# Two schedule lists of a fused attention and gated-MLP kernel: first scores at step 7, last splits from step 9

## The chip, the core and the metric

The kernel runs on one core of a Trainium2 chip. The metric is the device time of one execution in microseconds (us). The core's engines run their own instruction queues in order and wait for each other through semaphores: TensorE (PE, matrix products; PEld is its weight load), VectorE (DVE), ScalarE (ACT), GpSimd (POOL) and SyncE (SP), which here issues every DMA.

## What is computed

Three stages, one after the other. Packed attention: per batch (8) and head (8), 32 learned queries p attend to 576 keys, and then 576 queries q attend to the 32 results. A gated MLP with an RMS norm follows, and then a bilinear layer with two matrices behind it.

```python
p_packed = sm_attn(p, k, v)              # 32 rows per head
out = sm_attn(q, p_packed, p_packed)     # 576 rows per head
x = out as (4608, 512)
xn = x / rms(x) * rms_g
x = (silu(xn @ w_gate) * (xn @ w_val)) @ w_out
a = x @ w1
b = x @ w2
result = (a * b @ w3) @ w_out2
```

The large weights arrive as 64-bit numbers and are converted on the chip. Products that need more than one pass of the fast format are made from a high and a low part ("split": ACT rounds to the high part, DVE or POOL subtracts it to get the low one).

## The kernel before

The first stage is a loop over the 8 batches (`dense_units(b)`, line 362). A batch has 48 units, two to a tile of 128 rows and 288 columns of the hidden layer: an even unit is the gate, an odd unit the value. Each unit is six matmuls of 128x288 into one PSUM bank of a pool of four (tag `gv`, line 376). An even unit is then read by ACT (tanh, line 382, `th`) and by DVE (line 383); an odd unit is read by ACT (`vl`, line 387) and multiplied on POOL (`ht`, line 388). Groups of 8 units share one pair of weight tiles `wbh`/`wbl`; after the fourth unit of a group `wb_unit` (line 330) makes the next group's with 16 small matmuls (line 337) into a slot of the second PSUM pool (tag `at`, two slots of two banks), and splits it in two halves: ACT `wbh` (L55), DVE `wbl` (L56).

Other work is put between the units by hand. `planned(main, (steps, generator), ...)` (line 431) lets the main generator emit unit n, and then, for each list in which n stands, lets that list's generator emit its next piece. So a list entry n means: behind unit n and ahead of unit n+1 in the queue of every engine that the piece uses. In batch b these are:

- `pack(b + 2)` by the list `PACK` (for b = 0 to 5): its first piece emits all score matmuls of p and k (line 181) into two `at` slots, then for the first slot a maximum over the row (DVE, line 185), its scaling (DVE, line 186) and the exponential (ACT, line 188); its second piece does the same three for the second slot. The third piece, at step 16, transposes the result. The first two pieces issue no DMA.
- `unpack(b + 1)` by the list `UNPACK`: among others, a maximum (L272) at step 4, a subtraction (DVE, L274) and an exponential (ACT, L275) at step 6, and a sum with a reciprocal (DVE, L278 to L280) at step 11.
- conversions of weights (gate and value weights in batch 0, `w_out` after it, which are stored to a DRAM tile `wo_d`).

In the last batch (b = 7) there is no attention left; its one list drives `first_loads()` (line 516): at its first entry it fetches three of the twelve rows of `wo_d` (`fetch`, line 495; SP, line 497), and at each of the next twelve it splits one row into `wo_h`/`wo_l` (ACT L55; DVE or POOL in turn, L56) and fetches a further one, then the first rows of the hidden layer; the last two entries split those (`hh`/`hl`). After it come the output product (L566), the folded weights, and the bilinear layer in five passes (L811, L784).

Of the kernel before, what the change touches and what calls it, by code (L numbers as in the profile page):

```python
# [16 lines left out]
B, H, S, D = 8, 8, 576, 64  # L17
# [15 lines left out]
def packed_attention_swiglu_bilinear(ctx: ExitStack, tc, qT, kT, v, pT, rms_g, w_gv, w_out,  # L33
# [17 lines left out]
    def bank():  # L51
        return ps.tile([128, 512], F32, tag="gv", name="gv", bufs=4)

    def split(hi, lo, src, eng_lo):
        nc.scalar.activation(out=hi, in_=src, func=AF.Copy)  # L55
        eng_lo.tensor_tensor(out=lo, in0=src, in1=hi.bitcast(F32), op=ALU.subtract)  # L56
# [273 lines left out]
    def wb_unit(b, g):  # L330
        gP1T = res["gP1T", b]
        while not all((g, c) in converted for c in range(NC)):
            next(gvw)
        t = slot("at")
        for c in range(NC):
            for e in range(2):
                nc.tensor.matmul(t[32 * c:32 * c + 32, e, :], lhsT=gP1T[64 * e:64 * e + 64, c, :],  # L337
                                 rhs=wgv[64 * e:64 * e + 64, c, :, 256 * g:256 * g + 256],
                                 start=True, stop=True, tile_position=(64 * e, 32 * c), skip_group_check=True)
        hi = dp.tile([128, 2, 512], F32R, tag="wbh", name="wbh", bufs=2)  # L340
        lo = dp.tile([128, 2, 512], F32R, tag="wbl", name="wbl", bufs=2)
        for e in range(2):
            split(hi[:, e], lo[:, e], t[:, e], nc.vector)
        wb[b, g] = (hi, lo)
# [4 lines left out]
    def store_later(steps, **dma):  # L349
        held.append([steps, dma])  # L350

    def stores():
        for x in held:
            x[0] -= 1
        while held and held[0][0] <= 0:
            nc.sync.dma_start(**held.pop(0)[1])

    def flush():
        while held:
            stores()  # L360

    def dense_units(b):
        ah, al = res["a2n", b]
        for g in range(6):
            hi, lo = wb.pop((b, g))
            for f in range(2):
                ht = dp.tile([128, 2, HALF], F32, tag="ht", name="ht", bufs=3)
                for hf in range(2):
                    th = dp.tile([128, HALF], F32, tag="th", name="th", bufs=3)
                    vl = dp.tile([128, HALF], F32, tag="vl", name="vl", bufs=2)  # L370
                    for i in range(2):
                        t = bank()
                        n = 0
                        for w, x in ((hi, ah), (hi, al), (lo, ah)):
                            for e in range(2):
                                nc.tensor.matmul(t[:, :HALF],  # L376
                                                 lhsT=w[:, e, 256 * i + 128 * f:256 * i + 128 * f + 128],
                                                 rhs=x[:, e, HALF * hf:HALF * hf + HALF],
                                                 start=(n == 0), stop=(n == 5))
                                n += 1  # L380
                        if i == 0:
                            nc.scalar.activation(out=th, in_=t[:, :HALF], func=AF.Tanh, scale=0.5)  # L382
                            nc.vector.scalar_tensor_tensor(out=th, in0=th, scalar=1.0, in1=t[:, :HALF],  # L383
                                                           op0=ALU.add, op1=ALU.mult)
                            stores()
                            yield 0.75
                    nc.scalar.activation(out=vl, in_=t[:, :HALF], func=AF.Copy, scale=0.5)  # L387
                    nc.gpsimd.tensor_tensor(out=ht[:, hf], in0=th, in1=vl, op=ALU.mult)  # L388
                    if hf == 1:
                        store_later(4, out=hT_d[2 * g + f, :, S * b:S * b + S],  # L390
                                    in_=ht.rearrange("p a n -> p (a n)"))
                    yield 0.75
                    if f == 0 and hf == 1:
                        if g + 1 < 6:
                            wb_unit(b, g + 1)
                        elif b + 1 < B:
                            wb_unit(b + 1, 0)
# [5 lines left out]
    def drain(gen):  # L403
        for _ in gen:
            pass
# [25 lines left out]
    def planned(main, *others):  # L431

        for n, _ in enumerate(main):
            for at, gen in others:
                for _ in range(at.count(n)):
                    next(gen, None)
        for at, gen in others:
            for n in at:
                assert n < 60
            drain(gen)  # L440
# [19 lines left out]
        drain(front[x])  # L460
    ow = converting([(w_out[128 * i:128 * i + 128, :], wo_d[128 * i:128 * i + 128, :]) for i in range(NF)], out_weight)

    PACK = [8, 8, 16, 31, 32, 40, 43]
    UNPACK = [0, 1, 3, 4, 6, 11, 13, 15, 17, 24, 24, 25, 31, 32, 40, 41, 42, 44]
    for b in range(B - 1):
        others = [(UNPACK, unpack(b + 1))]
        if b + 2 < B:
            others.insert(0, (PACK, pack(b + 2)))
        if b == 0:
# [25 lines left out]
    def fetch(src):  # L495
        x = rot.tile([128, TT], F32, tag="hr", name="hr", bufs=5)
        nc.sync.dma_start(out=x, in_=src)
        return x
# [5 lines left out]
    def fetch_h(n):  # L504
        if n < len(hrows):
            t, kk = hrows[n]
            hts[n] = fetch(hT_d[kk, :, TT * t:TT * t + TT])

    def split_h(n):
        if n < len(hrows):  # L510
            hi = rot.tile([128, TT], F32R, tag="hh", name="hh", bufs=3)
            lo = rot.tile([128, TT], F32R, tag="hl", name="hl", bufs=3)
            split(hi, lo, hts[n], nc.vector)
            hts[n] = hi, lo

    def first_loads():
        rows = [wo_d[128 * kk:128 * kk + 128, :] for kk in range(NF)]
        ahead = [fetch(x) for x in rows[:3]]
        yield
        for i in range(NF):  # L520
            split(wo_h[:, i], wo_l[:, i], ahead.pop(0), nc.gpsimd if i % 2 else nc.vector)
            if i + 3 < NF:
                ahead.append(fetch(rows[i + 3]))
            else:
                fetch_h(i + 3 - NF)
            yield
        fetch_h(3)
        for n in range(2):
            split_h(n)
            yield  # L530

    planned(dense_units(B - 1), (list(range(0, 45, 3)), first_loads()))
    flush()
    dp_ctx.close()
    wraw_ctx.close()
# [363 lines left out]
```

## Time and profile before

| what | us |
| --- | --- |
| median of 3 runs | 1436.34 |
| lowest and highest run | 1432.2 and 1437.11 |
| the profiled execution's own time | 1431.36 |
| its span, first to last instruction | 1429.2 |
| PE busy in it | 1353.3 (95%) |
| DVE, ACT, POOL busy | 787.5, 545.7, 489.7 |

Of the profiled execution, 2.2 us lie around its span. The mean granted clock of TensorE over the span is 0.984 of full speed. Times in the rows are counted from the start of the span. Matmuls are pipelined, so that their ends are modelled and neighbours overlap in the records; the idle times given in rows are those between records.

### The profile page before, as it was taken

What the parts mean: (1) busy time and instruction counts of PE and PEld (TensorE: products, weight loads), DVE (VectorE), ACT (ScalarE), POOL (GpSimd) and SP (SyncE); (2) the same over time, 40 slices, a digit from 0 to 9 for tenths busy, and PEclk for the clock granted to TensorE, in tenths of its full rate; (3) what the DMA queues carried; (4) which work ended last, traced back from release to release, by engine and by line L of the source; (5) the groups of instructions that cost most, each with busy time, mean ns of one, the idle gap of its engine ahead of it and who ended that gap; (6) DMA issues with size and microseconds to landing.
All of it is one profiled execution on the core that took longest, in us unless ns stands there. A gap on an engine that the chain in (4) does not pass through costs nothing.

```text
span 1429.2 us, 22605 instructions
## 1 busy us (share of the span) xinstructions
PE 1353.3 (95%) x8824; PEld 1119.0 (78%) x8824; DVE 787.5 (55%) x1267; ACT 545.7 (38%) x1080; POOL 489.7 (34%) x438
## 2 busy tenths in 40 slices
PE   4579999999999899999999999999999999999988
PEld 2358878788788788888888877887888788788887
DVE  4787566766766547736177855335335343534443
ACT  3455455555555566525155542113112111211211
POOL 2456445445455452203034503322222222222111
PEclk9689999999999999999999999999999999999999
DMA  9853454443221357735369875434442643444263
GB/s 312 290 197 108 160 192 137 148 155 111 107 97 75 134 170 264 238 124 162 122 226 407 325 288 225 164 148 160 165 155 81 243 155 124 171 155 149 82 250 124
DMA packets 65562, 253.65 MB, mean 177 GB/s; under 512 B 7344, under 2 KB 7344, under 8 KB 55344
## 3 DMA queue, kind: packets, MB, share of 16 engines
q1 hardware_dynamic: 65456, 252.21, 49.8%
q8 instruction: 69, 1.13, 0.3%
q14 instruction: 37, 0.30, 0.1%
HBM read 185.08 MB, written 67.11 MB: 176 GB/s over the span
## 4 chain that ended last, share of the span: by engine, by line
PE 80%; DVE 7%; ACT 3%; DMA 3%; issue 2%; POOL 0%; SPq 0%; DVEq 0%; ACTq 0%; POOLq 0%
PE gv L811 24%; PE gv L376 17%; PE at L566 13%; PE gv L784 7%; PE at L784 7%; PE gv L566 5%; PE gv L658 3%; PE at L337 2%; DMA w<-ws_d 2%; DVE th L383 1%; PE at L292 1%; DVE a L274 1%; DVE wbl L56 1%; DVE wgv L112 1%; ACT vl L387 1%
## 5 line engine op out<-in xcount | busy, mean ns | idle before, releaser
L811 PE MATMUL gv<-xh,w 128*128 128x512 f32 (+1 forms) x1120 | 287.3, 371 | 10.1 <-DMA w<-ws_d 6.4
L55 ACT ACTIVATE hh<-hr 128x512 fp32r<-128x512 f32 (+1 forms) x148 | 91.0, 618 | 419.1 <-DVE hr L779 332.0
L811 PEld LDWEIGHTS gv<-xh,w 128*128 128x128 f32 x1120 | 201.1, 190 | 49.4 <-DMA w<-ws_d 7.6
L388 POOL TENSOR_TENSOR ht<-th,vl 128x288 f32<-128x288 f32 x192 | 163.7, 860 | 178.1 <-ACT vl L387 95.8
L376 PE MATMUL gv<-ah,wbh 128*128 128x288 f32 x768 | 178.7, 314 | 16.0 <-ACT vl L387 12.4
L376 PEld LDWEIGHTS gv<-ah,wbh 128*128 128x128 f32 x768 | 122.6, 190 | 67.6 <-issue 26.9
L838 POOL TENSOR_TENSOR u<-u,c 128x512 f32<-128x512 f32 (+1 forms) x40 | 63.9, 1598 | 319.9 <-DVE u L779 319.9
L376 PE MATMUL gv<-al,wbh 128*128 128x288 f32 x768 | 167.1, 298 | 0.0
L779 DVE TENSOR_TENSOR hr<-gv,hr 128x512 f32<-128x512 f32 (+1 forms) x80 | 51.0, 638 | 209.0 <-PE gv L811 209.0
L376 PE MATMUL gv<-ah,wbl 128*128 128x288 f32 x768 | 165.2, 296 | 0.0
L56 DVE TENSOR_TENSOR hl<-hr,hh 128x512 fp32r<-128x512 f32 (+1 forms) x148 | 130.2, 883 | 60.3 <-ACT hh L55 57.7
L811 PE MATMUL gv<-xl,w 128*128 128x512 f32 (+1 forms) x560 | 161.4, 370 | 0.0
L114 POOL TENSOR_TENSOR c_o<-c_o,c_y 128x512 int32<-128x512 int32 x52 | 73.9, 1421 | 206.6 <-DVE c_o L112 193.6
L376 PEld LDWEIGHTS gv<-al,wbh 128*128 128x128 f32 x768 | 125.2, 190 | 1.1 <-DVE al L56 0.9
L376 PEld LDWEIGHTS gv<-ah,wbl 128*128 128x128 f32 x768 | 124.4, 190 | 0.0
L383 DVE SCALAR_TENSOR_TENSOR th<-th,gv 128x288 f32<-128x288 f32 x192 | 84.3, 444 | 63.1 <-ACT th L382 62.2
L811 PEld LDWEIGHTS gv<-xl,w 128*128 128x128 f32 x560 | 102.1, 190 | 18.3
L566 PE MATMUL at<-hl,wo_h 128*128 128x512 f32 x288 | 112.3, 390 | 0.9 <-DVE hl L56 0.8
L566 PE MATMUL at<-hh,wo_h 128*128 128x512 f32 x288 | 112.2, 390 | 0.0
L566 PE MATMUL at<-hh,wo_l 128*128 128x512 f32 x288 | 112.1, 389 | 0.0
L387 ACT ACTIVATE vl<-gv 128x288 f32<-128x288 f32 x192 | 79.4, 414 | 58.6 <-PE gv L376 56.1
L56 DVE TENSOR_TENSOR wbl<-at,wbh 128x512 fp32r<-128x512 f32 x96 | 65.9, 686 | 60.4 <-ACT wbh L55 59.8
(125 smaller groups left out, 2341.9 us busy)
## 6 DMA issues: line engine op xcount, KB each, us to landing
w<-ws_d SPq DMA_DIRECT2D x40, 1792.0 KB, 7.5
hT_d<-ht SPq DMA_DIRECT2D x96, 288.0 KB, 2.7
hr<-hT_d SPq DMA_DIRECT2D x108, 256.0 KB, 4.7
ws_d<-stage SPq DMA_DIRECT2D x16, 896.0 KB, 8.6
w<-in_w_gv_dram SPq DMA_DIRECT2D x24, 512.0 KB, 7.0
w<-in_w_out_dram SPq DMA_DIRECT2D x20, 512.0 KB, 4.4
v<-in_v_dram SPq DMA_DIRECT2D x8, 1152.0 KB, 7.5
q<-in_qT_dram SPq DMA_DIRECT2D x8, 1152.0 KB, 7.1
```

The costliest lines, as they stand in the source:

```text
L55: nc.scalar.activation(out=hi, in_=src, func=AF.Copy)
L56: eng_lo.tensor_tensor(out=lo, in0=src, in1=hi.bitcast(F32), op=ALU.subtract)
L114: nc.gpsimd.tensor_tensor(out=d, in0=d, in1=shape(y), op=ALU.add)
L376: nc.tensor.matmul(t[:, :HALF], lhsT=w[:, e, 256 * i + 128 * f:256 * i + 128 * f + 128], rhs=x[:, e, HALF * hf:HALF * hf + HALF], start=(n ...
L383: nc.vector.scalar_tensor_tensor(out=th, in0=th, scalar=1.0, in1=t[:, :HALF], op0=ALU.add, op1=ALU.mult)
L387: nc.scalar.activation(out=vl, in_=t[:, :HALF], func=AF.Copy, scale=0.5)
L388: nc.gpsimd.tensor_tensor(out=ht[:, hf], in0=th, in1=vl, op=ALU.mult)
L566: nc.tensor.matmul(acc[m], lhsT=w[:, kk, 128 * m:128 * m + 128], rhs=x, start=(kk == 0 and a == 0), stop=(kk == NF - 1 and a == 2))
L779: nc.vector.tensor_tensor(out=out, in0=a, in1=b, op=op)
L784: nc.tensor.matmul(acc[m], lhsT=x[:, 128 * m:128 * m + 128], rhs=w[i], start=(i == 0 and n == 0), stop=(i == 7 and n == 2))
L811: nc.tensor.matmul(t, lhsT=wi[:, r, j, a], rhs=x[b][:, j, r, :w], start=(start and n == 0), stop=(n == 5), skip_group_check=True)
L838: nc.gpsimd.tensor_tensor(out=u2, in0=u2, in1=c22, op=ALU.mult)
```

## The change

Two lists change. In `PACK` the first two pieces of `pack` move from step 8 to step 7, that is from behind the even unit 8 to ahead of it. In the last batch the list of `first_loads` keeps its first entry at 0 and its 15 entries, but the others are 9, 11, 14, 17, 19, 22, 25, 28, 30, 33, 36, 38, 41 and 44 in place of 3, 6, 9, ... 42. No instruction is added or removed.

```diff
-    PACK = [8, 8, 16, 31, 32, 40, 43]
+    PACK = [7, 7, 16, 31, 32, 40, 43]
...
-    planned(dense_units(B - 1), (list(range(0, 45, 3)), first_loads()))
+    planned(dense_units(B - 1), ([0, 9, 11, 14, 17, 19, 22, 25, 28, 30, 33, 36, 38, 41, 44], first_loads()))
```

## Rows read from the trace of the kernel before

**Rows 1.** Table by stretch: us, busy time of PE, PEld, DVE, ACT, POOL, granted clock, DMA.

```profile
78.00:86.00 8.00, 5.29 (x44) 3.58 (x45) 6.38 (x10) 4.16 (x10) 3.34 (x3) 0.57 0.55 168
...
136.00:424.00 288.00, 279.27 (x2996) 233.58 (x2995) 187.31 (x384) 153.10 (x363) 139.14 (x154) 1.00 0.42 139
...
484.00:488.60 4.60, 0.18 (x2) 0.00 (x0) 1.78 (x3) 2.24 (x6) 0.00 (x0) 1.00 0.90 300
488.60:492.00 3.40, 3.27 (x13) 3.27 (x14) 1.40 (x4) 1.60 (x5) 2.71 (x3) 0.50 0.37 133
492.00:527.00 35.00, 35.00 (x291) 30.81 (x291) 19.23 (x33) 24.55 (x58) 23.04 (x25) 1.00 0.50 157
```

**Rows 2.** Waits in the last batch (476.2 to 527.3): total us, times, longest.

```profile
PE gv L376 <- ACT vl L387: 4.5, 1, 4.5
...
ACT wo_h L55 <- DMA hr<-wo_d: 5.2, 1, 5.2
```

**Rows 3.** Timeline of ACT, last batch: start, us, operation [idle before <- releaser].

```profile
479.89 0.41 ACT L387 ACTIVATE vl<-gv 128x288 f32<-128x288 f32 x1 [0.45 <-PE gv L376]
485.49 0.63 ACT L55 ACTIVATE wo_h<-hr 128x512 fp32r<-128x512 f32 x1 [5.19 <-DMA hr<-wo_d]
486.03 0.58 ACT L55 ACTIVATE wbh<-at 128x512 fp32r<-128x512 f32 x1
...
488.26 0.42 ACT L387 ACTIVATE vl<-gv 128x288 f32<-128x288 f32 x1
```

**Rows 4.** Timeline of SP's DMA issues, last batch.

```profile
480.58 0.32 SPq L356 DMA_DIRECT2D wo_d<-c_o  x1
482.73 4.46 SPq L497 DMA_DIRECT2D hr<-wo_d  x6
```

**Rows 5.** PE by line, batches 1 to 5: busy, mean | idle before <- releasers.

```profile
L376 PE MATMUL gv<-ah,wbh 128*128 128x288 f32 x481 | 111.3, 312 | 3.1 <-ACT vl L387 3.0
...
L337 PE MATMUL at<-wgv,gP1T 64*32 64x512 f32 x480 | 32.7, 601 | 5.7 <-ACT e L188 5.5
```

**Rows 6.** The same for batch 0.

```profile
L376 PE MATMUL gv<-ah,wbh 128*128 128x288 f32 x96 | 23.8, 331 | 7.9 <-ACT vl L387 4.4 <-DVE th L383 3.5
...
L337 PE MATMUL at<-wgv,gP1T 64*32 64x512 f32 x96 | 6.5, 600 | 2.2 <-ACT e L188 1.2 <-DVE a L266 1.0
```

**Rows 7.** Timeline of PE, units 8 to 16 of batch 5.

```profile
376.29 0.42 PE L376 MATMUL gv<-ah,wbh 128*128 128x288 f32 x2
...
377.17 1.20 PE L181 MATMUL at<-k,pTs 64*32 64x288 f32 x32
...
381.96 1.09 PE L337 MATMUL at<-wgv,gP1T 64*32 64x512 f32 x16 [1.00 <-ACT e L188]
...
387.04 0.54 PE L376 MATMUL gv<-ah,wbh 128*128 128x288 f32 x2 [0.61 <-ACT vl L387]
```

**Rows 8.** Timeline of DVE, the same stretch.

```profile
375.51 0.69 DVE L56 TENSOR_TENSOR wbl<-at,wbh 128x512 fp32r<-128x512 f32 x1 [0.66 <-ACT wbh L55]
...
377.51 0.75 DVE L274 TENSOR_TENSOR a<-a,mx 128x576 f32<-128x576 f32 x1
...
380.05 0.75 DVE L185 TENSOR_REDUCE mx<-at 128x1 f32<-128x576 f32 x1
...
383.47 0.46 DVE L383 SCALAR_TENSOR_TENSOR th<-th,gv 128x288 f32<-128x288 f32 x1 [1.63 <-ACT th L382]
```

**Rows 9.** Timeline of ACT, the same stretch.

```profile
378.29 0.69 ACT L275 ACTIVATE a<-a 128x576 f32<-128x576 f32 x1 [1.90 <-DVE a L274]
...
381.08 0.74 ACT L188 ACTIVATE e<-at,nb 128x576 f32<-128x576 f32 x1 [1.51 <-DVE nb L186]
...
382.67 0.40 ACT L387 ACTIVATE vl<-gv 128x288 f32<-128x288 f32 x1
...
386.57 0.42 ACT L387 ACTIVATE vl<-gv 128x288 f32<-128x288 f32 x1
```

**Rows 10.** Line 274, all 16: duration in ns, least, median, most.

```profile
L274 DVE TENSOR_TENSOR a<-a,mx x16: 749/751/1765, 32.5 to 435.0; 128x576 f32<-128x576 f32 x16
```

## The prediction

> **What bounds the kernel now.** I read the table of stretches first. In batches 1 to 5 PE is busy for 279.3 of 288.0 us, at a granted clock of 1.00 [rows 1]: this stage is bound by PE, and what can be won there is the 8.7 us in which PE stands still. The table of PE by line says what these are: 5.7 us lie ahead of the small matmuls of line 337, released by the exponential of `pack`, and 3.1 us ahead of a gate unit, released by a copy `vl` [rows 5], so about 1.1 and 0.6 us in each of five batches. The reader should see the same two stops in each batch, not a spread of small ones. The last batch has one large stop instead: in the 4.6 us from 484.0 PE works 0.18 us, and in the 3.4 us behind it the granted clock is 0.50, the lower of its two levels, where all stretches around have 1.00 [rows 1]. The list of waits gives that stop to `vl` (4.5 us, once), but the larger wait, 5.2 us, is that of ACT for a row of `wo_d` [rows 2]; PE only waits for what stands behind it on ACT.
>
> **The last batch, step by step.** The first split is emitted at step 3, ahead of the two `wbh` of the next group and of tanh and `vl` of units 4 and 5. ACT ends the `vl` of unit 3 at 480.30, then waits until 485.49, and only then come `wbh` (486.03) and the `vl` of unit 5 (to 488.68), on which unit 8 starts [rows 3]. The row is late because SP stores the last of `wo_d` at 480.58 and issues the fetch at 482.73 [rows 4]. The change leaves that fetch at step 0, behind the same store, so the row still lands at about 485.4. What it moves is the split: from step 3 to step 9, and the later splits with it, each with the fetch that it issues on SP.
>
> Without the split in front, `wbh` is limited by line 337 alone and can start about 0.5 us behind the `vl` of unit 3, at 480.8 in place of 486.03: 5.2 us earlier. The `vl` of unit 5 then ends at 488.68 - 5.2 = 483.5. Today unit 8 starts at 488.7, right behind that `vl`, so PE has done unit 7 at 488.7 - 4.5 = 484.2, and unit 8 starts without a stop: 4.5 us won. ACT reaches the split of step 9 behind `vl` of unit 9. Unit 8 takes 0.88 us on PE by its start and that of the work behind it [rows 7]; records on PE overlap by some 0.2 us, so two such units from 484.0 end at 485.8, `vl` ends at about 486.1, and the row has been there since 485.4: cover of 0.7 us. The low clock goes with the stop: 3.4 us at half speed are 1.7 us of work lost. I take 4.5 + 1.7 = **6.2 us**, with ends of 4.5 (the clock falls all the same) and 6.2.
>
> The other splits now come every two or three units, not every three. On PE's path that costs nothing as long as ACT keeps up: in 492 to 527 ACT is busy 24.6 of 35.0 us with some ten splits in it, PE 35.0 of 35.0 [rows 1], and 12 splits in 29 units in place of 33 add about an eighth to their share, 0.63 us each [rows 3]. The fetch of a row is three splits ahead of its use, six units or more, against the 2.7 us from issue to landing of the first. SP's stores of `ht` lie between these fetches as before. The last two pieces move from steps 39 and 42 to 41 and 44; three units, 2.6 us, are left behind the last one for one split.
>
> **Batches 1 to 5.** I work batch 5 through; the others have the same two stops. Today unit 8 starts at 376.29, the scores at 377.17 [rows 7]; DVE ends its subtraction at 378.26, then stands until tanh of unit 8 and takes the row maximum only at 380.05 [rows 8]; ACT starts the exponentials at 381.08 and the second gives way to `vl` of unit 9 at 382.67 [rows 9]. Line 337 waits for the slot that the first exponential frees, and starts at 381.96, 1.00 late.
>
> With the pieces at step 7 the scores take unit 8's place at 376.29. Their second slot is freed by `wbl`, which ends at 376.20 [rows 8], so they start at once, with 0.1 us in hand. They end 1.2 us later, and DVE goes from the subtraction straight into the maximum at 378.2 in place of 380.05. From maximum to exponential it is 381.08 - 380.05 = 1.03 us, so the exponentials start at 379.2, just as ACT is done with line 275 (to 378.98) and one `vl`. They take 382.67 - 381.08 = 1.6 us, to 380.8. The first slot is free at about 380.1 and PE has done its units at 381.96 - 1.00 = 380.96, so the stop of 1.00 is gone. What ACT did before is now behind: tanh of unit 8, 0.3 us. `vl` of unit 9 starts at 381.1 in place of 382.67, 1.6 us earlier. The chain from there (tanh and line 383 of unit 10, sum and reciprocal, `wbl`, second `wbh`, `vl` of unit 13) keeps its order, so that `vl`, which ends at 386.99 [rows 9], ends at 385.4. PE wants unit 16 at 387.04 - 0.61 - 1.00 = 385.43: the second stop is gone too, but for a tenth. **1.6 us in each, 8.0 us in five**, with ends of 0 (the stops come back elsewhere) and 8.7.
>
> What is queued behind the moved pieces: tanh of unit 8 on ACT, line 383 of unit 8 on DVE. The latter now ends at about 381.1 + 0.1 + 0.46 = 381.7, and the bank that it frees is wanted by one of units 12 and 13, of which the first starts 1.0 us behind line 337, at 381.9. That is the thinnest cover of the sum, 0.2 us. POOL and SP get nothing from the two pieces.
>
> **Batch 0** has stops of 1.2 us ahead of line 337 behind the exponential, of 4.4 us behind `vl` and 3.5 us behind line 383 [rows 6], and stands at a granted clock of 0.57 from 78 to 86 [rows 1]. The 4.4 us come before step 7 and stay. The same 1.6 us as above come off the chain that follows. I take **1.6 us**, with ends of -1.7 (one more stretch at the low clock, the price of the one at 488.6) and 3.5. Batch 6 has no `pack`: nothing.
>
> The sum is 6.2 + 8.0 + 1.6 = 15.8 us. Against the profiled execution's 1431.36 that gives 1415.6. The median of the runs shown is 1436.34, 5 us above it; the same sum from there is **1420.5**, which I predict.
>
> One rule of the skill speaks against the second part. Rows first: line 274 takes 0.75 us in the median, but 1.77 once [rows 10]. The Trainium skill, "SBUF — State Buffer", section "Who interferes with whom", says that a VectorE tensor_tensor with both inputs in SBUF and a GpSimd operation share one port pair, and that the one that comes second is blocked for the whole instruction. Line 274 is such an operation, and it now stands directly ahead of the row maximum. The trace has the long one once in 16, so it is a rival with a small chance below; were it the rule in every batch, the sum would be 5 us smaller.
>
> **The rivals.**
> - *The stops move instead of going.* Tanh and line 383 of unit 8 are now behind two exponentials and two maxima; if they end 1 us later than worked out, unit 12 waits for its bank as long as line 337 did, and unit 16 as before. For it: the cover of 0.2 us. Against it: DVE's 1.63 us of idle time ahead of the next line 383 [rows 8], which gives room. Then only the last batch's 6.2 us are won: 1430.
> - *The last batch gives less.* The row lands later than 486.1, or the next rows do, and ACT stops at step 9 with tanh of unit 10 behind it; or the clock falls anyway. Some 4 us less: 1424.5. Against it: the store and fetch ahead of it are untouched [rows 4].
> - *Line 274 is drawn out* to 1.77 us in batches 1 to 5: everything behind it is 1.0 us late, `vl` of unit 13 too, and 0.6 us of 1.6 is left in each: 1425.5.
> - *Slower.* ACT falls behind PE for good: scores that wait for the slot of `wbl` (0.1 us of cover) delay maxima, exponentials, and with them tanh of unit 8 and every `vl` behind it, and unit 8 now stands behind the scores on PE. In six batches this has to cost (15.8 + 7.2) / 6 = 3.8 us each, more than is won, for a time over 1443.5. It decides from `wbl` ending 3.8 us later than now; nothing in the change delays `wbl` of that group.
>
> **Chances.** A measurement can tell about 0.5%, 7.2 us, from no change. Forecast 0.78, moved stops 0.09, less in the last batch 0.05, line 274 0.05, slower 0.03. The first rival lies within 0.5%, the two next to it are faster by more, so faster 0.88, same 0.09, slower 0.03. The range goes down to 1412 (the lowest 1431.4 less 6.2, 8.7 and 3.5 is 1413; one stretch of low clock in batch 0 gone as well, 1.7, about 1412) and up to 1429, which takes in all but the stops that move and slower.
>
> **What would show it.** Right: no stop of PE over 0.3 us ahead of line 337 or units 12 and 16 in batches 1 to 5, the maximum of line 185 directly behind line 274 on DVE, no wait of ACT for `wo_d` over 0.5 us, granted clock 1.00 from 100 to 527. Wrong: a new stop of PE ahead of unit 12 or 13 released by DVE line 383; a wait of ACT for `hr` at step 9; a longer stretch of low clock in batch 0.

## The result and the profile after

The changed kernel takes 1419.22 us in the median of 4 runs (1414.79 to 1420.32), against 1434.27 us of the kernel before in the same comparison. The ratio is 0.9891, with a 95% interval of 0.9868 to 0.9915: 15.1 us or 1.1% faster. The prediction was 1420.5 us, from a sum of 15.8 us.

The profiled execution took 1419.24 us, its span is 1417.5 us. Table by stretch (us, busy time of PE, PEld, DVE, ACT, POOL, granted clock, DMA) of the changed kernel: batches 1 to 5, and the last batch in two parts.

```profile
136.00:417.00 281.00, 279.01 (x2997) 233.89 (x2996) 188.20 (x384) 153.17 (x364) 138.91 (x154) 1.00 0.43 143
...
469.00:477.00 8.00, 8.00 (x67) 6.85 (x67) 5.40 (x10) 5.42 (x13) 4.83 (x6) 1.00 0.23 80
477.00:514.00 37.00, 37.00 (x306) 32.72 (x305) 20.86 (x37) 26.20 (x62) 26.18 (x27) 1.00 0.63 198
```

Against [rows 1], the reader should see that batches 1 to 5 stand still for 2.0 of 281.0 us (8.7 of 288.0 before), and the last batch not at all, with the clock at 1.00 throughout. PE by line in batches 1 to 5, as in [rows 5]: the stop ahead of line 337 is gone, and 1.8 of the 3.1 us of idle time ahead of unit 16 are left.

```profile
L376 PE MATMUL gv<-ah,wbh 128*128 128x288 f32 x480 | 110.8, 312 | 1.8 <-ACT vl L387 1.8
...
L337 PE MATMUL at<-wgv,gP1T 64*32 64x512 f32 x480 | 32.7, 601 | 0.2
```

The same stretch of batch 5 as in [rows 7 to 9], in the changed kernel; first the timeline of PE (start, us, operation, [idle before <- releaser]). The scores start at 370.61, so that 5.68 us added to one of these times gives its place in the working of the prediction (376.29).

```profile
370.61 1.20 PE L181 MATMUL at<-k,pTs 64*32 64x288 f32 x32
...
375.11 1.09 PE L337 MATMUL at<-wgv,gP1T 64*32 64x512 f32 x16
...
378.61 0.43 PE L376 MATMUL gv<-ah,wbh 128*128 128x288 f32 x2
...
379.86 0.53 PE L376 MATMUL gv<-ah,wbh 128*128 128x288 f32 x2 [0.28 <-ACT vl L387]
```

The timeline of DVE there:

```profile
371.74 0.75 DVE L274 TENSOR_TENSOR a<-a,mx 128x576 f32<-128x576 f32 x1
372.41 0.75 DVE L185 TENSOR_REDUCE mx<-at 128x1 f32<-128x576 f32 x1
...
375.53 1.05 DVE L383 SCALAR_TENSOR_TENSOR th<-th,gv 128x288 f32<-128x288 f32 x2 [1.33 <-ACT th L382]
376.50 0.75 DVE L278 TENSOR_REDUCE rs<-a 128x18 f32<-128x576 f32 x1
377.29 0.44 DVE L279 TENSOR_SCALAR rs<-rs 128x18 f32<-128x18 f32 x1
...
377.94 0.63 DVE L56 TENSOR_TENSOR wbl<-at,wbh 128x512 fp32r<-128x512 f32 x1
```

And of ACT:

```profile
373.44 0.74 ACT L188 ACTIVATE e<-at,nb 128x576 f32<-128x576 f32 x1
...
375.32 0.41 ACT L387 ACTIVATE vl<-gv 128x288 f32<-128x288 f32 x1
...
379.38 0.42 ACT L387 ACTIVATE vl<-gv 128x288 f32<-128x288 f32 x1
```

DVE goes from the subtraction straight into the maximum (371.74 + 0.75, then 372.41), the exponential follows at 373.44, line 337 has no idle time ahead of it, and unit 16 still waits 0.28 us for `vl`. In the last batch ACT now does `wbh` and `vl` of unit 5 at once, and reaches the first split at 479.00 without waiting; SP's store and fetch stand where they did, relative to the batch (compare [rows 3, 4]). Timeline of ACT in the last batch:

```profile
472.72 0.41 ACT L387 ACTIVATE vl<-gv 128x288 f32<-128x288 f32 x1 [0.45 <-PE gv L376]
473.75 0.60 ACT L55 ACTIVATE wbh<-at 128x512 fp32r<-128x512 f32 x1 [0.62 <-PE at L337]
...
475.88 0.42 ACT L387 ACTIVATE vl<-gv 128x288 f32<-128x288 f32 x1
...
478.70 0.41 ACT L387 ACTIVATE vl<-gv 128x288 f32<-128x288 f32 x1 [0.44 <-PE gv L376]
479.00 0.62 ACT L55 ACTIVATE wo_h<-hr 128x512 fp32r<-128x512 f32 x1
```

Timeline of SP's DMA issues there:

```profile
473.41 0.32 SPq L356 DMA_DIRECT2D wo_d<-c_o  x1
475.56 1.75 SPq L497 DMA_DIRECT2D hr<-wo_d  x4
```

To compare kernels by stage, the start of each batch's first matmul is taken from the traces, for the two kernels and those of the experiments below. Times in us; "behind" is what follows the last matmul of the last batch.

| kernel | ahead of batch 0 | batch 0 | 1 to 5 | 6 | last | behind | span |
| --- | --- | --- | --- | --- | --- | --- | --- |
| before | 63.9 | 72.4 | 288.3 | 51.6 | 51.2 | 901.8 | 1429.2 |
| changed | 65.3 | 71.1 | 281.1 | 51.6 | 45.0 | 903.4 | 1417.5 |
| pack_only | 64.2 | 71.1 | 281.2 | 51.6 | 52.5 | 899.6 | 1420.2 |
| last_only | 64.2 | 72.3 | 288.4 | 51.6 | 45.0 | 901.3 | 1422.8 |
| pack_7_8 | 65.4 | 73.9 | 287.4 | 51.6 | 51.8 | 901.7 | 1431.7 |
| weights_early | 64.5 | 73.9 | 288.4 | 52.8 | 45.7 | 902.0 | 1427.4 |
| last_from_6 | 64.7 | 73.9 | 288.1 | 51.6 | 45.1 | 901.2 | 1424.6 |
| pack_6_6 | 65.6 | 70.3 | 285.0 | 51.6 | 51.3 | 902.3 | 1426.1 |
| sum_at_12 | 65.0 | 73.4 | 278.0 | 52.9 | 45.0 | 900.2 | 1414.5 |
| changed_again | 65.2 | 71.1 | 280.9 | 51.6 | 45.1 | 901.2 | 1415.2 |
| sum_at_12_inner | 65.1 | 71.1 | 277.9 | 51.6 | 45.1 | 899.9 | 1410.7 |

The three stages that the change touches give 1.3 + 7.2 + 6.2 = 14.7 us. In these two profiles the stages that it doesn't touch took 1.4 us more ahead of batch 0 and 1.6 us more at the end, so that the spans differ by 11.7 us only; the medians over the runs differ by 15.1. An untouched stage moves by 1 to 4 us from one profile to the next, which is why each verdict below rests on the stage in question first, and on the total second.

### The profile page after: what moved, and what is told of

It reads as the page before. It is cut to its first block, busy times and chain, and to the rows that moved or that the text cites. A ratio compares the mean times of both kernels' runs of the same rounds, so it can differ in the third digit from the quotient of the medians.

```text
span 1417.5 us, 22608 instructions
## 1 busy us (share of the span) xinstructions
PE 1354.0 (96%) x8824; PEld 1119.6 (79%) x8824; DVE 790.6 (56%) x1267; ACT 545.0 (38%) x1080; POOL 489.2 (35%) x438
## 4 chain that ended last, share of the span: by engine, by line
PE 82%; DVE 5%; DMA 3%; ACT 2%; issue 2%; SPq 0%; POOL 0%; DVEq 0%; ACTq 0%; POOLq 0%
PE gv L811 23%; PE gv L376 19%; PE at L566 13%; PE gv L784 7%; PE at L784 7%; PE gv L566 5%; PE gv L658 3%; DMA w<-ws_d 3%; PE at L337 3%; PE at L292 1%; DVE wgv L112 1%; PE at L208 1%; DVE th L383 1%; DMA ws_d<-stage 1%; DVE wbl L56 1%
## 5 line engine op out<-in xcount | busy, mean ns | idle before, releaser
L383 DVE SCALAR_TENSOR_TENSOR th<-th,gv 128x288 f32<-128x288 f32 x192 | 84.4, 445 | 54.8 <-ACT th L382 51.8
## 6 DMA issues: line engine op xcount, KB each, us to landing
hT_d<-ht SPq DMA_DIRECT2D x96, 288.0 KB, 3.0
```

## Experiments

**Each part alone.** First the scores, with the old list in the last batch:

```diff
-    PACK = [8, 8, 16, 31, 32, 40, 43]
+    PACK = [7, 7, 16, 31, 32, 40, 43]
```

> First scores at step 7, splits of the last batch as before. If the two parts are independent and each works through its own queue, batches 0 to 5 are shorter by 8.5 us in sum (1.3 in batch 0, 1.4 in each of the five) and the last batch keeps its stop of 4.5 us and the low clock behind it: about 8.5 us faster than before, ratio 0.994. If the gain of the scores hangs on the other part, or belongs to it, there is no difference: 1.000.

Measured: 1423.68 us against 1434.0, ratio 0.9932 (0.9911 to 0.9952). Batches 1 to 5 take 281.2 us, as in the changed kernel, batch 0 1.2 us less: 8.3 us, where about 8.5 were expected. The last batch keeps its stop, and there the stretch at the low clock is longer than in [rows 1]; table by stretch behind the stop:

```profile
480.00:485.20 5.20, 4.49 (x19) 4.49 (x20) 2.07 (x5) 3.12 (x9) 3.45 (x4) 0.51 0.50 144
485.20:488.00 2.80, 2.80 (x24) 1.68 (x24) 1.15 (x2) 0.82 (x2) 0.73 (x2) 0.69 0.70 231
```

Then the last batch alone:

```diff
-    planned(dense_units(B - 1), (list(range(0, 45, 3)), first_loads()))
+    planned(dense_units(B - 1), ([0, 9, 11, 14, 17, 19, 22, 25, 28, 30, 33, 36, 38, 41, 44], first_loads()))
```

> The splits of the last batch from step 9, first scores at step 8 as before. Independent parts: the last batch goes from 51.2 to 45.0 us (4.5 of stop, 1.7 of low clock), batches 0 to 5 stay, about 6.2 us faster, ratio 0.996. If the clock falls for another reason than the stop, 4.5 us and a stretch at half clock remains in the last batch.

Measured: 1425.64 us against 1434.0, ratio 0.9943 (0.9926 to 0.9961). The last batch takes 45.0 us, batches 0 to 5 are as before. The same part of the last batch as in [rows 1], which there held the stop and the low clock:

```profile
484.00:488.60 4.60, 4.60 (x44) 3.61 (x42) 2.40 (x5) 3.03 (x8) 2.46 (x4) 1.00 0.93 292
488.60:492.00 3.40, 3.40 (x33) 3.39 (x26) 1.92 (x4) 2.54 (x7) 2.03 (x3) 1.00 0.80 263
```

The clock term of the sum is thereby shown: no stop, no low clock. The product of the two ratios is 0.9875; the changed kernel has 0.9891 (0.9868 to 0.9915), so the two parts add up within what can be measured.

**Is it the slot, or the chain through ACT?** Only the first piece of `pack` moves:

```diff
-    PACK = [8, 8, 16, 31, 32, 40, 43]
+    PACK = [7, 8, 16, 31, 32, 40, 43]
```

> Only the first piece (scores, first maximum and exponential) moves to step 7, the second stays at step 8; the last batch as before. If what counts is the chain of exponentials through ACT up to the vl of unit 13, the first exponential frees the slot early, so the stop ahead of line 337 (1.0 us) goes, but the second maximum stands behind line 383 of unit 8, vl of unit 9 comes as late as before, and the stop ahead of unit 16 grows from 0.6 to about 1.6 us: batches 1 to 5 stay at 57.5 us, ratio 1.000. If what counts is the slot alone, 1.0 us goes in each batch: 5 to 6 us faster, ratio 0.996.

Measured: 1433.16 us, ratio 0.9995 (0.9983 to 1.0008); batches 1 to 5 take 287.4 us (288.3 before). PE by line in batches 1 to 5, and the stop ahead of unit 16 in batch 5:

```profile
L376 PE MATMUL gv<-ah,wbh 128*128 128x288 f32 x480 | 111.3, 313 | 6.7 <-ACT vl L387 6.6
...
L337 PE MATMUL at<-wgv,gP1T 64*32 64x512 f32 x480 | 32.7, 601 | 0.2
```

```profile
389.09 0.53 PE L376 MATMUL gv<-ah,wbh 128*128 128x288 f32 x2 [1.27 <-ACT vl L387]
```

The idle time of 5.7 us ahead of line 337 is gone but for 0.2, and that ahead of line 376 has grown from 3.1 to 6.7 us. The stage is 0.9 us shorter, the total the same within its interval. This is the first rival of the prediction made real, though at unit 16 and not at unit 12: the place where PE stops moved, and next to nothing was won. What has to come earlier is the second exponential, because `vl` of unit 9 and the whole chain up to `vl` of unit 13 stand behind it on ACT.

**Is it the row's lateness?** The split stays at step 3, and the row comes earlier, because the last conversion of `w_out` is made inside batch 6:

```diff
-            others.append(([21, 35], some(ow, 2)))
+            others.append(([21, 35], some(ow, 2)) if b < B - 2 else ([14, 21, 35], some(ow, 3)))
```

> Both lists as before; the twelfth conversion of w_out is made inside batch 6 (entries 14, 21 and 35 in place of 21 and 35) and no longer behind it, so that the last store of wo_d is out before the last batch begins. If the stop of the last batch is the late row alone, the row lands some 4 to 5 us earlier, the split at step 3 finds it, and the last batch takes 45 to 46 us with the clock at 1.00, 5 to 6 us faster, ratio 0.996, with no split moved. If the split itself at step 3 is what delays wbh (0.6 us on ACT), a stop of 0.5 to 1 us stays; if the fetch waits for something else than the store, the stop of 4.5 us stays, ratio 1.000.

Measured: 1429.12 us, ratio 0.9966 (0.9953 to 0.9978). The last batch takes 45.7 us in place of 51.2, at full clock, with no split moved; batch 6 pays 1.2 us for the conversion. Timeline of ACT in the last batch:

```profile
483.34 0.41 ACT L387 ACTIVATE vl<-gv 128x288 f32<-128x288 f32 x1 [0.44 <-PE gv L376]
484.95 0.63 ACT L55 ACTIVATE wo_h<-hr 128x512 fp32r<-128x512 f32 x1 [1.20 <-DMA hr<-wo_d]
485.49 0.58 ACT L55 ACTIVATE wbh<-at 128x512 fp32r<-128x512 f32 x1
```

Timeline of SP's DMA issues around its start:

```profile
473.49 8.43 SPq L356 DMA_DIRECT2D hT_d<-ht  x3
482.10 4.56 SPq L497 DMA_DIRECT2D hr<-wo_d  x6
```

The row is still waited for, but 1.20 us and not 5.19: the fetch goes out at 482.10, 2.5 us into the batch (6.6 before), now behind the last store of `ht`, which takes the place of the store of `wo_d` in SP's queue. A stop of 0.56 us is left on PE, ahead of unit 8; timeline of PE:

```profile
488.20 0.53 PE L376 MATMUL gv<-ah,wbh 128*128 128x288 f32 x2 [0.56 <-ACT vl L387]
```

So the long stop was the late row: an earlier row removes all but this rest, a later split all of it. Whether the rest comes from the 1.20 us of waiting or from the 0.63 us of the split itself, which still stands ahead of `wbh`, this run does not separate.

**How late must the split be?** As the change, but with the first split at step 6:

```diff
-    planned(dense_units(B - 1), (list(range(0, 45, 3)), first_loads()))
+    planned(dense_units(B - 1), ([0, 6, 11, 14, 17, 19, 22, 25, 28, 30, 33, 36, 38, 41, 44], first_loads()))
```

> The lists of the kernel before, but the splits of the last batch at 0, 6, 11, 14, 17 and on: as the change has them, the first one at step 6 instead of 9. ACT gets there about 1.6 us ahead of the row and waits. If what cost the stop was that wbh and vl of unit 5 stood behind the waiting split, this wait delays only vl of unit 7 and what follows it, which has four banks of cover: the last batch takes 45.0 to 45.5 us, the clock stays at 1.00. If each us that ACT waits is one that PE stands still, it takes 46.6 us.

Measured: the last batch takes 45.1 us (1426.34 us in all, a single run). ACT waits 1.56 us for the row, with `vl` of unit 7 behind it, and PE has no idle time in the whole batch. Timeline of ACT:

```profile
485.15 0.42 ACT L387 ACTIVATE vl<-gv 128x288 f32<-128x288 f32 x1
...
487.50 0.63 ACT L55 ACTIVATE wo_h<-hr 128x512 fp32r<-128x512 f32 x1 [1.56 <-DMA hr<-wo_d]
488.04 0.39 ACT L387 ACTIVATE vl<-gv 128x288 f32<-128x288 f32 x1
```

PE by line in the last batch (its largest group; the idle time is the last number):

```profile
L376 PE MATMUL gv<-ah,wbh 128*128 128x288 f32 x96 | 21.5, 305 | 0.0
```

So it is not the wait of ACT as such that costs, but what is queued behind it: 1.20 us with `wbh` behind them left PE a stop of 0.56 us (weights_early), 1.56 us with only `vl` of unit 7 and what follows it behind them left none. At step 6 the first split is as free as at step 9.

**One step earlier for the scores.**

```diff
-    PACK = [8, 8, 16, 31, 32, 40, 43]
+    PACK = [6, 6, 16, 31, 32, 40, 43]
```

> The first scores at step 6, one unit earlier than in the change; the last batch as before. If the slot that wbl frees sets the earliest time for the scores, PE stops 0.7 to 0.8 us ahead of them in batches 1 to 5, vl of unit 7 comes late behind three exponentials (another 0.3 us ahead of unit 11), and the stop ahead of unit 16 is gone: 56.7 to 57.1 us each, between the kernel before (57.5 to 57.9) and the change (56.1 to 56.4). If earlier is simply better, 55.8 us or less.

Measured: 285.0 us for batches 1 to 5, 57.0 each (1428.18 us in all, a single run), as the first theory has it. The stop ahead of the scores looks small, though. PE by line in batches 1 to 5, and the scores in the timeline of PE in batch 5:

```profile
L376 PE MATMUL gv<-ah,wbh 128*128 128x288 f32 x480 | 110.7, 312 | 1.7 <-ACT vl L387 1.7
...
L181 PE MATMUL at<-k,pTs 64*32 64x288 f32 x160 | 9.3, 408 | 0.8 <-DVE wbl L56 0.5
```

```profile
372.40 1.96 PE L181 MATMUL at<-k,pTs 64*32 64x288 f32 x32
```

0.8 us of idle time stand ahead of the scores in all five batches, but the 32 matmuls take 1.96 us from the first to the last where they take 1.20 in the changed kernel: most of the wait lies behind the first one or two of them, inside what the table calls busy. These 0.76 us are about what the stage loses against the changed kernel, 3.9 us in five batches; the stop ahead of unit 16 is gone as expected, and the 1.7 us ahead of line 376 are the expected 0.3 us ahead of unit 11 in each batch.

**What is left ahead of unit 16.** On the changed kernel, the sum of the next batch moves from between the last gate unit and the split of the new weights to behind that split, and POOL's multiplication by it (L281) with it:

```diff
-    UNPACK = [0, 1, 3, 4, 6, 11, 13, 15, 17, 24, 24, 25, 31, 32, 40, 41, 42, 44]
+    UNPACK = [0, 1, 3, 4, 6, 12, 13, 15, 17, 24, 24, 25, 31, 32, 40, 41, 42, 44]
```

> The changed kernel, and in it the first sum and reciprocal of the next batch (L278 to L280, 1.4 us on DVE) move from step 11 to step 12, that is behind the split of the new weights. If the stop that is left ahead of unit 16 (0.28 to 0.49 us in batches 1 to 5, 2.6 us in batch 0) comes through DVE by line 383 of units 8 and 10, this sum and wbl, it goes: batches 1 to 5 take 55.8 to 55.9 us each, batch 0 about 1.3 us less, some 3 us in all. If it comes from ACT being full, it stays, and the sum that is late only delays the transposes behind it.

Measured: 1415.96 us, ratio 0.988 (0.9859 to 0.9901). Batches 1 to 5 take 278.0 us, 3.1 less than the changed kernel, 55.6 each: more than expected, and the stop is gone. PE by line in batches 1 to 5:

```profile
L376 PE MATMUL gv<-ah,wbh 128*128 128x288 f32 x480 | 110.2, 311 | 0.0
```

The records show 1.8 us of idle time for what is left in the changed kernel, and 3.1 us are won. Idle time between records is less than a stop costs, since records of neighbours overlap; the starts of the units tell more. In batch 5 unit 16 starts 1.56 us behind unit 15 before (387.04 in [rows 7], 385.48 below), 1.25 in the changed kernel (379.86 - 378.61, above), and 0.79 here. Timeline of PE, unit 15 of the kernel before:

```profile
385.48 0.43 PE L376 MATMUL gv<-ah,wbh 128*128 128x288 f32 x2
```

Units 15 and 16 of sum_at_12:

```profile
378.11 0.43 PE L376 MATMUL gv<-ah,wbh 128*128 128x288 f32 x2
...
378.90 0.43 PE L376 MATMUL gv<-ah,wbh 128*128 128x288 f32 x2
```

PE by line in batch 6:

```profile
L376 PE MATMUL gv<-ah,wbh 128*128 128x288 f32 x96 | 22.0, 311 | 1.6 <-ACT vl L387 1.6
```

Batch 6 pays for it with a new stop of 1.1 us (1.6 in sum with the 0.5 that it had), and batch 0, whose stop ahead of unit 16 fell from 2.6 to 1.3 us, has a new one of 1.7 us ahead of unit 19. Hence the move in batches 1 to 5 alone, beside the changed kernel on the same chip:

```diff
-        others = [(UNPACK, unpack(b + 1))]
+        late = UNPACK[:5] + [12] + UNPACK[6:]
+        others = [(late if 0 < b < B - 2 else UNPACK, unpack(b + 1))]
```

> The changed kernel with the first sum and reciprocal at step 12 only in batches 1 to 5, where the run before showed no stop left. If batch 6's new stop of 1.1 us ahead of unit 19 and batch 0's of 1.7 us there came from this move, they are gone, batch 6 takes 51.6 us again, and batches 1 to 5 keep 55.6: about 3 us under the changed kernel, ratio to the kernel before 0.987, to the changed one 0.998. If the stops in batches 0 and 6 have another cause, they stay and nothing more is won than with the move everywhere.

> The changed kernel itself, on the chip of the next run, for a direct comparison: 0.989 of the kernel before, batches 1 to 5 of 56.1 to 56.4 us.

Measured: 1413.68 us, ratio to the kernel before 0.9861 (0.9841 to 0.988); the changed kernel beside it 1418.3 us, 0.9889 (0.9871 to 0.9906). Batch 6 is back at 51.6 us, batches 1 to 5 take 277.9. The stages give 3.0 us, the medians 4.6; the two intervals overlap by a little, so the total by itself does not settle it, but the stage does. It is the fastest version of this study.

## Why the prediction was right

- *The last batch, 6.2 us.* Measured 6.2. Row, wait and queue were as read: weights_early shows that the stop is the late row, last_from_6 that it costs only through what stands behind it on ACT, last_only that the low clock goes with it. The size of the clock term holds for this profile of the kernel before; the same stop cost 1.2 us more in pack_only. The cover of the first split, worked out at 0.7 us, held: ACT comes to it at 479.00, 3.4 us behind the fetch's issue at 475.56, against the 2.7 us to landing of [rows 3, 4].
- *Batches 1 to 5, 1.6 us in each, 8.0 in five.* Measured 7.2, 1.4 in each. The first stop went as worked out: from scores to exponential 2.83 us (2.9 in the working), to `vl` of unit 9 4.71 us (4.8). The mis-sized term is the second stop, "gone too, but for a tenth": 0.28 to 0.49 us of idle time is left in each batch, and in three of the five (0.49, 0.32, 0.43, the others 0.28) it breaks the prediction's own sign of being right, no stop over 0.3 us ahead of unit 16.

  Two things were wrong in the step. PE wants unit 16 earlier than worked out, 8.97 us behind the scores (379.86 - 0.28 - 370.61) and not 9.14 (385.43 - 376.29): the working put the scores at the very start of unit 8, and took 1.00 us of idle time between records for the whole lateness of line 337. And the chain from `vl` of unit 9 to `vl` of unit 13 does not keep its length: it is 3.90 us in [rows 9] (386.57 - 382.67) and 4.06 here (379.38 - 375.32). Line 383 of unit 8, which used to be done by then, now runs on DVE directly ahead of that of unit 10 (two in 1.05 us from 375.53), but DVE comes to the sum no later for it: L278 starts 1.17 us behind `vl` of unit 9 before (383.84) and 1.18 here (376.50). The 0.16 us are L279's, 0.28 us before and 0.44 here (the last section has its rows); that line 383 causes this by way of POOL is argued there, not shown. The cover of 0.2 us for the bank of unit 12 held. sum_at_12 shows that the stop hangs on this chain: with 1.4 us of DVE work taken out of it, the stop is gone.

  That 7.2 came so near 8.0 is in part luck. Without either stop the five batches take 278.0 us, 10.3 less than before, where the prediction took the 8.7 us of idle time as the most to be won; and 3.1 of the 10.3 were left, not half a us. The two errors go against each other.

Timeline of DVE in batch 5 of the kernel before, the sum:

```profile
383.84 0.75 DVE L278 TENSOR_REDUCE rs<-a 128x18 f32<-128x576 f32 x1
```

- *Batch 0, 1.6 us.* Measured 1.3 against the kernel before, and 1.2 in pack_only, but not by the way that was worked out. The stop behind the exponential is gone, as forecast. The stop of 4.4 us, which the prediction placed before step 7, stands ahead of unit 8, directly ahead of the scores; in the changed kernel the scores come first and wait 4.0 us for `wbl` there. And the stops behind line 383, which are on the chain that should have become shorter, are 3.8 us where [rows 6] has 3.5. The spread of batch 0 is as large as the gain: its code is the same in last_only and last_from_6, which took 72.3 and 73.9 us. So no run shows this term, and that its size came out is luck.

Timeline of PE in batch 0 of the kernel before:

```profile
80.70 0.85 PE L376 MATMUL gv<-ah,wbh 128*128 128x288 f32 x2 [4.38 <-ACT vl L387]
...
82.44 2.17 PE L181 MATMUL at<-k,pTs 64*32 64x288 f32 x32
```

Waits of PE in batch 0 of the changed kernel: total us, times, longest.

```profile
PE at L181 <- DVE wbl L56: 4.0, 1, 4.0
PE gv L376 <- DVE th L383: 3.8, 2, 2.6
```

- *The rivals.* That the stops only move was the right rival to fear: pack_7_8 is a case of it, and one list entry decides between the two. Line 274 was drawn out, but by little: directly ahead of the row maximum it took 0.92 us in batch 1 and 0.86 in batch 4, 0.75 in the three others, and the stop ahead of unit 16 was 0.49 and 0.43 us in these two. The prediction read [rows 10] as 1.77 us "once", but that row gives only the longest: in the kernel before, 4 of the 16 took 1.16 to 1.77 us, in the changed kernel 5 took 0.86 to 1.77, and each of these started while POOL was at work and ended 0.61 or 0.62 us after POOL's operation. The trace agrees here with the rule of the Trainium skill ("SBUF — State Buffer", "Who interferes with whom"), and what decides the cost is whether POOL is at work when line 274 starts; it was not the 1.0 us in every batch of the rival. The slower case did not come near: in pack_6_6 the scores do wait for the slot of `wbl`, and it costs 0.8 us per batch against the change, not 3.8.

Line 274 in batch 1 of the changed kernel, timeline of DVE, and the multiplication beside it, timeline of POOL (it ends at 147.06, line 274 at 147.67):

```profile
146.75 0.92 DVE L274 TENSOR_TENSOR a<-a,mx 128x576 f32<-128x576 f32 x1
```

```profile
146.25 0.81 POOL L388 TENSOR_TENSOR ht<-th,vl 128x288 f32<-128x288 f32 x1 [3.42 <-DMA hT_d<-ht]
```

## What to carry to other kernels

Where an order is written by hand, a piece that waits costs through what stands behind it on its engine: move it behind the work that the bottleneck needs next, and the same wait is free. When a stop is removed, follow the chain on to the next wait of the bottleneck engine before counting the gain; half a move can shift the stop at no gain. Count a stop by the starts of the work around it, since the idle time between matmul records came out too small here (8.8 us for 10.3). Judge such edits by the stage that they touch, since untouched stages of one and the same code differ by 1 to 4 us.

## What the runs showed that was not expected

- The same stop of 4.5 us ahead of unit 8 of the last batch was followed by 3.4 us at the granted clock of 0.50 in the kernel before, and by about twice that in pack_only (rows above), where the last batch took 1.2 us more. It is 3.4 us in pack_6_6 too, and 6.8 in pack_7_8.
- Ten stops of 0.6 to 1.4 us in 288 us left the granted clock at 1.00 in the kernel before [rows 1, 5]. The Trainium skill, "TensorE: Matmul & The Clock Gate", section "A second HAM failure mode: psum-queue depth-cycling", tells of another kernel, where short idle spells between groups of matmuls made the clock swing; none of it is seen in these batches.
- L279, a DVE operation on 18 numbers a partition, ends when a multiplication on POOL beside it ends. In the changed kernel POOL's pair of `ht` ends at 377.69 and L279 at 377.73 (its row stands in the timeline of DVE above); timeline of POOL:

```profile
376.12 1.57 POOL L388 TENSOR_TENSOR ht<-th,vl 128x288 f32<-128x288 f32 x2 [1.73 <-ACT th L382]
```

In the kernel before, the pair ended at 384.87 and L279 at 384.90; timeline of POOL:

```profile
383.14 1.73 POOL L388 TENSOR_TENSOR ht<-th,vl 128x288 f32<-128x288 f32 x2 [2.99 <-ACT vl L387]
```

And DVE's L279 there:

```profile
384.62 0.28 DVE L279 TENSOR_SCALAR rs<-rs 128x18 f32<-128x18 f32 x1
```

Over all 16, its least duration is 0.18 us, its median 0.28 us before and 0.42 us in the changed kernel. The traces of all the runs here bear it out: of 176 executions of L279, 153 start while an operation runs on POOL, and each of these ends 0.03 to 0.04 us after that operation; the other 23 take 0.18 us. No run changed POOL's work alone. Why POOL's pair ends later in the changed kernel is argued: `ht` of unit 9 needs `th` of unit 8, which line 383 now finishes late, and the pair starts 0.80 us behind `vl` of unit 9 (376.12 - 375.32) where it was 0.47 (383.14 - 382.67).
